# Token mixing of batches two to four by seven products of sums, with the sums of the weights made in the first batch

## The chip, the cores and the metric

The kernel runs on one core of a Trainium2 chip. The metric is the time of one execution on the device in microseconds (us). Five engines work side by side, each with a queue of its own that it takes in order: TensorE (PE in the profile; PEld are its weight loads), VectorE (DVE), ScalarE (ACT), GpSimd (POOL) and SyncE (SP), which here issues all transfers between DRAM and the on-chip memory SBUF. Matrix products are summed up in the eight banks of PSUM.

## The reference

Clustered attention for 4 batches, 8 heads, 768 tokens and 64 values a head gives `x` (4 x 768 x 512). The change concerns what follows:

```python
theta = x @ w_theta                       # 512 x 512
zr, zi = x * np.cos(theta), x * np.sin(theta)
yr = np.einsum('ts,bsd->btd', w_tok_r, zr)   # w_tok_r, w_tok_i: 768 x 768
yi = np.einsum('ts,bsd->btd', w_tok_i, zi)
u = x + yr + yi
return u + np.maximum(u @ w_ch, 0.0)      # w_ch: 512 x 512
```

## The kernel before

The first part, 447 us long, is attention: 16 pairs of heads in an order written out by hand (`todo`, `in_order`). It also turns the 64-bit weights into 32 bits (`early_weights`). The second part, the one changed, goes through the batches. It is recorded in program order, and a scheduler then sets the order on each engine.

All products are made in fp32r from a rounded part and its residue: ScalarE casts to the high part, GpSimd (or VectorE) subtracts it for the low part, and TensorE sums three products, high by high, high by low, low by high.

- `theta(b, t)`: for 128 tokens (tile t of 6), 12 products of 512 columns into bank `tp` (L659), then on VectorE `kk`, `r` (L665 to L667), a turned copy `xn` of x (L652), ScalarE's absolute value and sines (L670, L924), VectorE's products with x (L926), the casts (L929) and GpSimd's subtractions (L931). Result: zr, zi with high and low parts, 128 tokens x 512.
- `mix(b, t)` (L980): for each of four blocks of 128 channels and for r and i, three products with the high or low part of the weight tile's 768 columns, cut in two at the bank's edge, 48 products in all. y (512 channels x 768 tokens) fills six banks over the six tiles. In the last batch the columns go in parts of 256 (72 products a tile), and the last two tiles are done part by part, so that its channel stage starts early.
- `add_y` (L991 to L994): x + y on VectorE, cast and residue for u. `channel` (L1003, L1008): 8 blocks of 12 products of 384 columns, ReLU and sum on VectorE, the result to DRAM.

Theta runs two tiles ahead of mix. During the first batch also `late()` works: it brings back the weight tiles 3 to 5 (`kept`, residues L893) and turns `w_ch` into 32 bits in four pieces `wtmp` (L142 to L153, casts L165, residues L166).

Of the kernel before, what the change touches and what calls it, by code (L numbers as in the profile page):

```python
# [22 lines left out]
PW = 256  # L23
TAIL = 2
# [19 lines left out]
def kernel(  # L44
# [112 lines left out]
    def split_w(hi, lo, src, cols, new, eng, most, kept=None):  # L157

        def chunk(sl):
            w = yield from to_f32(src[:, sl], sl.stop - sl.start, new)  # L160
            yield
            if kept is not None:
                nc.sync.dma_start(out=kept[:, sl], in_=w)
                return
# [17 lines left out]
    w_d = {(t, x): dram.tile([P, S], F32, name=f"wd{t}{x}") for t in range(EARLY, NT) for x in "ri"}  # L182
# [80 lines left out]
    def f(ap):  # L263
        return ap.bitcast(F32)
# [336 lines left out]
    def first_rotation():  # L601

        xs = ma[0].tile([P, NCT, P], F32, tag="ab", name="xs")
# [3 lines left out]
        xh, xl, xn, kk, r = rotation_tiles(0, "0_0")  # L607
# [12 lines left out]
    def rotation_tiles(n, name):  # L620
        pool = ma[n % 2]
        xh = pool.tile([P, NCT, P], F32R, tag="xh", name=f"xh{name}")
# [3 lines left out]
        return xh, xl, xn, kk, pool.tile([P, DM], F32, tag="r", name=f"r{name}")  # L626
# [35 lines left out]
    def rotation_reduce(n, name, tp, kk, r):  # L662
# [3 lines left out]
        nc.vector.scalar_tensor_tensor(out=r, in0=kk, scalar=-C1, in1=tp, op0=ALU.mult, op1=ALU.add)  # L666
        nc.vector.scalar_tensor_tensor(out=r, in0=kk, scalar=-C2, in1=r, op0=ALU.mult, op1=ALU.add)  # L667
# [177 lines left out]
    pm = mctx.enter_context(tc.tile_pool(name="pm", bufs=2, space=PSUM))  # L845
    py = mctx.enter_context(tc.tile_pool(name="py", bufs=1, space=PSUM))
    mx = mctx.enter_context(tc.tile_pool(name="mx", bufs=2))
    ma.append(mctx.enter_context(tc.tile_pool(name="ma1", bufs=1)))
    mz = mctx.enter_context(tc.tile_pool(name="mz", bufs=3))
    m2 = mctx.enter_context(tc.tile_pool(name="m2", bufs=2))  # L850
    m1 = mctx.enter_context(tc.tile_pool(name="m1", bufs=1))
    m0 = mctx.enter_context(tc.tile_pool(name="m0", bufs=1))

    def mbank(name):
        return pm.tile([P, 512], F32, tag="bank", name=name)
# [10 lines left out]
    def load_x(b):  # L866
        xT = mx.tile([P, NP, S], F32, tag="xT", name=f"xT{b}")
# [4 lines left out]
        else:  # L872
            with tc.issue_after(last_load[0].ins):
# [238 lines left out]
```

## Time and profile before

| | us |
|---|---|
| median of 3 runs (780.78 to 781.37) | 780.91 |
| the profiled execution | 783.62 |
| its span in the profile | 781.8 |
| TensorE busy in it | 772.4 |
| VectorE busy | 553.1 |
| GpSimd busy | 493.3 |
| ScalarE busy | 389.2 |
| attention ends, first mix begins, near | 449.5 |
| channel stage of the first batch ends | 531.4 |

The profile shows one execution. Rows of a timeline or of the chain of waits begin with start and duration in us; a group of instructions has line, engine, operation, result and sources, count, busy time in us and the mean in ns. Busy matmuls overlap in the records, so TensorE's pace is read from the chain, where the pieces follow each other without overlap. The chain is the work that ended last, followed back.

### The profile page before, as it was taken

Reading aid. Unit: us, or ns where it says so; the run is one execution under the profiler, and the core shown is the slowest. Engines: PE = TensorE matmul, PEld = TensorE weight load, DVE = VectorE, ACT = ScalarE, POOL = GpSimd, SP = SyncE. Lnnn points to the kernel's source line nnn. Section 1 sums busy time; section 2 is a strip of 40 time slices with the busy share of each in tenths; the row PEclk is TensorE's granted clock in tenths of the full one; section 3 lists DMA queues with packets and bytes.
Section 4 is the critical chain, followed back from the end, with each engine's and each line's share of the span. In section 5 each row is a group of like instructions: output and inputs, shape, how many; then the busy total and the mean of one; then the engine's idle time right before and its main releaser. Section 6 shows DMA issues by size and latency. Waiting matters only on the chain.

```text
span 781.8 us, 14392 instructions
## 1 busy us (share of the span) xinstructions
PE 772.4 (99%) x5580; PEld 571.6 (73%) x5580; DVE 553.1 (71%) x689; ACT 389.2 (50%) x781; POOL 493.3 (63%) x289
## 2 busy tenths in 40 slices
PE   8999999999999999999998999999999999999998
PEld 6666566656666665666664588898889988899998
DVE  7788999999899989999899577854344444533322
ACT  3566766676767666666655555432333132503310
POOL 4568888989999999988986575461225112422231
PEclk9999999999999999999999999999999999999999
DMA  4123323433343334333453476124101411120001
GB/s 143 42 60 100 113 77 113 137 109 97 120 140 107 102 115 144 124 108 129 131 201 115 104 198 193 28 56 147 27 14 28 162 28 28 17 92 15 1 21 62
DMA packets 82592, 73.23 MB, mean 94 GB/s; under 512 B 59538, under 2 KB 66844, under 8 KB 82140
## 3 DMA queue, kind: packets, MB, share of 16 engines
q1 hardware_dynamic: 82524, 72.32, 31.2%
q8 instruction: 44, 0.72, 0.4%
q14 instruction: 24, 0.20, 0.1%
HBM read 56.89 MB, written 15.31 MB: 92 GB/s over the span
## 4 chain that ended last, share of the span: by engine, by line
PE 87%; DVE 6%; DMA 3%; ACT 2%; issue 1%; SPq 1%; POOL 0%; DVEq 0%; ACTq 0%
PE sc L411 26%; PE y L980 20%; PE av L559 17%; PE tp L659 6%; PE cy L1003 5%; PE m L411 4%; PE cp L1003 3%; PE sm L526 2%; PE lg L287 2%; DMA wtmp<-in_w_ch_dram 1%; PE y L1003 1%; PE lt L300 1%; DVE nm L433 1%; PE mt L441 1%; PE idle L228 1%
## 5 line engine op out<-in xcount | busy, mean ns | idle before, releaser
L487 ACT ACTIVATE at<-sc 128x384 f32<-128x384 f32 x384 | 174.0, 493 | 96.3 <-PE sc L411 52.4
L433 DVE TENSOR_REDUCE nm<-m 128x1 f32<-128x768 f32 x192 | 180.2, 947 | 26.0 <-PE m L411 24.5
L498 POOL TENSOR_TENSOR acc<-at,at 128x768 f32<-128x768 f32 x64 | 126.0, 1969 | 37.5 <-ACT at L487 37.5
L411 PE MATMUL m<-hk,hq 64*128 64x384 f32 x384 | 147.4, 384 | 0.2 <-DVE nm L433 0.2
L559 PE MATMUL av<-at,vt 128*64 128x384 f32 x768 | 146.4, 502 | 0.2 <-ACT xt L574 0.2
L498 POOL TENSOR_TENSOR acc<-acc,at 128x768 f32<-128x768 f32 x64 | 132.5, 2070 | 10.0 <-ACT at L487 8.0
L931 POOL TENSOR_TENSOR zlc<-ab,zhc 128x512 fp32r<-128x512 f32 x24 | 32.4, 1351 | 158.5 <-ACT zhc L929 157.0
L411 PE MATMUL m<-mk,mq 64*128 64x384 f32 x384 | 128.2, 334 | 0.1
L411 PE MATMUL sc<-hq,hk 64*128 64x384 f32 x384 | 116.7, 390 | 1.1 <-ACT at L487 1.1
L411 PEld LDWEIGHTS sc<-hq,hk 64*128 64x128 f32 x384 | 55.1, 183 | 63.5 <-issue 25.3
L411 PE MATMUL sc<-hq,lk 64*128 64x384 f32 x384 | 97.1, 335 | 0.0
L411 PE MATMUL sc<-mq,mk 64*128 64x384 f32 x384 | 97.0, 335 | 0.0
L411 PE MATMUL sc<-lq,hk 64*128 64x384 f32 x384 | 96.7, 335 | 0.0
L559 PEld LDWEIGHTS av<-at,vt 128*64 128x64 f32 x768 | 46.8, 137 | 59.4 <-issue 54.1
L411 PEld LDWEIGHTS m<-hk,hq 64*128 64x128 f32 x384 | 70.4, 183 | 2.0 <-DVE nm L433 1.4
L411 PEld LDWEIGHTS m<-mk,mq 64*128 64x128 f32 x384 | 71.1, 185 | 0.8 <-DVE mk L376 0.4
L665 DVE TENSOR_SCALAR kk<-tp 128x512 int32<-128x512 f32 x24 | 16.4, 685 | 76.5 <-PE tp L659 76.5
L502 DVE TENSOR_TENSOR acc<-acc,acc 128x768 f32<-128x768 f32 x30 | 63.9, 2130 | 0.0
L632 ACT CAST xh<-xT 128x512 fp32r<-128x512 f32 x23 | 14.2, 619 | 95.8 <-PE tp L659 91.6
L994 POOL TENSOR_TENSOR ul<-xT,uh 128x384 fp32r<-128x384 f32 (+1 forms) x36 | 33.5, 959 | 35.5 <-ACT uh L993 33.8
L411 PEld LDWEIGHTS sc<-mq,mk 64*128 64x128 f32 x384 | 54.3, 185 | 0.0
L411 PEld LDWEIGHTS sc<-hq,lk 64*128 64x128 f32 x384 | 54.1, 185 | 0.0
(177 smaller groups left out, 1699.3 us busy)
## 6 DMA issues: line engine op xcount, KB each, us to landing
vt<-in_v_dram SPq DMA_DIRECT2D x16, 384.0 KB
rb<-sd SPq DMA_DIRECT2D x32, 192.0 KB
xT_d<-xt SPq DMA_DIRECT2D x16, 384.0 KB
xb<-xT_d SPq DMA_DIRECT2D x96, 64.0 KB
rawq<-in_qT_dram SPq DMA_DIRECT2D x15, 384.0 KB
rawk<-in_kT_dram SPq DMA_DIRECT2D x15, 384.0 KB
w<-in_wrT_dram SPq DMA_DIRECT2D x6, 768.0 KB
xT<-xT_d SPq DMA_DIRECT2D x3, 1536.0 KB
```

The source lines that it names most:

```text
L411: nc.tensor.matmul(out, lhsT=stat[r, cols], rhs=mov[r, over], start=start, stop=stop)
L433: nc.vector.tensor_reduce(out=s["nm", a][:, j, i // 2:i // 2 + 1], in_=s["m", j][:, :, 0:HS], op=ALU.max, axis=AX.XY, negate=True)
L487: last_exp[0] = nc.scalar.activation(out=s["at", a, i][:, j], in_=s["sc", j], func=AF.Exp, scale=SCALE)
L498: last_acc[0] = nc.gpsimd.tensor_tensor(out=s["acc", a, x], in0=prev, in1=at, op=ALU.add)
L502: nc.vector.tensor_tensor(out=s["acc", a, 0], in0=s["acc", a, 0], in1=s["acc", a, 1], op=ALU.add)
L559: nc.tensor.matmul(s["av"][64 * j:64 * j + 64], lhsT=s["vt"][:, i, j, :], rhs=s["at", a, i][:, j], start=(i == 0), stop=(i == NT - 1))
L659: nc.tensor.matmul(tp, lhsT=xx[:, c, :], rhs=w_th[c][k], start=(n == 0), stop=(n == 3 * NCT - 1))
L665: nc.vector.tensor_scalar_mul(kk, tp, INV_2PI)
L931: nc.gpsimd.tensor_tensor(out=zl, in0=tr, in1=zh.bitcast(F32), op=ALU.subtract)
L980: last_mix[0] = nc.tensor.matmul(y_at(b, d, c0, c1), lhsT=zz[:, d * P:(d + 1) * P], rhs=ww[:, c0:c1], start=first and lead, stop=last, ski ...
L994: nc.gpsimd.tensor_tensor(out=ul[:, d, :], in0=x, in1=uh[:, d, :].bitcast(F32), op=ALU.subtract)
L1003: nc.tensor.matmul(cp, lhsT=w_c[d][k][:, e * P:(e + 1) * P], rhs=uu[:, d, :], start=(n == 0), stop=(n == 3 * NCT - 1), skip_group_check=True)
```

## The change

Per tile and batch the mixing is y = Wr zr + Wi zi. With channels and token columns each cut in two, it is a product of two by two blocks, and from the second batch on it is made by Strassen's seven products in place of eight. The first batch stays as it was.

- *Sums of weights.* For every weight tile, `make_forms(t)` loads the 32-bit weights from DRAM (`w_d`, now stored for all six tiles in attention), makes five sums on VectorE, seven casts on ScalarE and seven residues (five on GpSimd, two on VectorE). The seven forms (128 x 768: high and low halves of 384 columns) go where parts of the weights used up by the first batch stood. It is called for tile 4 behind the first batch's mix of tile 0, for 5 and 0 behind tile 2, for 1 and 2 behind tiles 3 and 4, for tile 3 behind the channel stage. The forms of tiles 4, 5 and 0 are also stored in DRAM and loaded in each batch (`load_forms`), tile 4 into the buffers of u, tile 5 into the place of tile 0.
- *Sums of z.* `split_z(b, t, h)` for each half h of the channels (256): three sums on VectorE, two casts, two residues on GpSimd. The second half waits in DRAM (`z_d`) until the first half's mix is done.
- *Products.* `mix_forms`: 7 forms x 3 products of 384 columns for a tile and half. Product four goes to a bank of its own, the six others to the banks of y. `add_products`: seven instructions on VectorE add them to x, once per half.
- *Channel stage.* `split_u_part` makes u's first half on GpSimd during the second half's mix, the second half behind `add_products` on VectorE; the products are taken in two steps, for the two halves. The last batch's parts of 256 columns (`PW`, `TAIL`) go.
- *Loads and buffers.* One buffer for x in place of two; theta's columns (`load_columns`) come by loads of their own; two z buffers in place of three; x of the next batch is loaded behind the channel stage.

The diff, cut to its core:

```diff
-            for w, src in ((w_r, wrT), (w_i, wiT)):
-                yield from split_w(*w[t], src[t * P:(t + 1) * P], S, raw_pair, nc.gpsimd, CKE)
+            for w, src, x in ((w_r, wrT, "r"), (w_i, wiT, "i")):
+                yield from split_w(
+                    *w[t], src[t * P:(t + 1) * P], S, raw_pair, nc.gpsimd, CKE, kept=w_d[t, x])
...
+    ORDER = (4, 3, 1, 5, 2, 6, 7)
...
+    KEPT = (4, 5, 0)
...
+    def make_forms(t):
+        raw = u_tile(f"raw{t}").rearrange("p c s -> p (c s)").bitcast(F32)
+        for x, k in enumerate("ri"):
+            nc.sync.dma_start(out=raw[:, x * S:(x + 1) * S], in_=w_d[t, k])
...
+        for x, m in enumerate(ORDER):
+            to = subs[PLACE[t][x]]
+            hi, lo = to[:, 0:HS], to[:, HS:S]
+            p, op, q = W_SUM[m]
+            src = part[:, p]
+            if op is not None:
+                src = part[:, 1] if m == 6 else sums[:, {4: 0, 3: 1, 1: 2, 7: 3}[m]]
+                nc.vector.tensor_tensor(out=src, in0=part[:, p], in1=part[:, q], op=op)
+            nc.scalar.copy(out=hi, in_=src)
+            (nc.vector if x in (1, 4) else nc.gpsimd).tensor_tensor(out=lo, in0=src, in1=f(hi), op=ALU.subtract)
+            if t in KEPT:
+                nc.sync.dma_start(out=w_f[t][:, m - 1], in_=f(to))
+
+    def load_forms(t):
+        for m in ORDER:
+            nc.sync.dma_start(out=f(forms[t][m]), in_=w_f[t][:, m - 1])
+
+    def split_z(b, t, h):
...
+            src = mzb.tile([P, 2, HD], F32, tag="zb", name=f"zb{b}_{t}")
+            nc.sync.dma_start(out=src, in_=z_d.pop((b, t)))
...
+        nc.vector.tensor_tensor(out=sums[:, 0:HD], in0=c[:, 0:HD], in1=s[:, 0:HD], op=ALU.add)
+        nc.vector.tensor_tensor(out=sums[:, HD:3 * P], in0=c[:, 0:P], in1=s[:, P:HD], op=ALU.add)
...
+        nc.vector.tensor_tensor(
+            out=parts[:, 1:n + 1:n - 1], in0=src[:, :, P:HD], in1=src[:, :, 0:P], op=ALU.subtract)
+        for cols, of in ((slice(0, 3 * P), sums), (slice(3 * P, 7 * P), src[:, :, 0:HD])):
...
+            nc.scalar.copy(out=h_, in_=of)
+            nc.gpsimd.tensor_tensor(out=l_, in0=of, in1=f(h_), op=ALU.subtract)
...
+    def mix_forms(tiles, first, last):
+        for m in ORDER:
+            cols = slice(Z_AT[m] * P, (Z_AT[m] + 1) * P)
+            for x, (t, (zh, zl)) in enumerate(tiles):
+                hi, lo = forms[t][m][:, 0:HS], forms[t][m][:, HS:S]
+                for k, (zz, ww) in enumerate(((zh, hi), (zh, lo), (zl, hi))):
+                    nc.tensor.matmul(
+                        product(m), lhsT=zz[:, cols], rhs=ww, start=first and x == k == 0,
+                        stop=last and x == len(tiles) - 1 and k == 2, skip_group_check=True)
+
+    def add_products(b, h):
...
+        add(x[:, 0:3:2], twice(4), ALU.add)
+        add(x[:, 1:4:2], twice(3), ALU.subtract)
+        add(x[:, 0:4:3], twice(1), ALU.add)
+        add(x[:, 0:4:3], y[:, 2:4, 0:HS], ALU.subtract)
+        add(x[:, 1:3], y[:, 2:4, 0:HS], ALU.add)
...
+    made = {0: (4,), 2: (5, 0), 3: (1,), 4: (2,)}
+    for t in range(NT):
+        theta(*divmod(t + AHEAD, NT))
...
+        mix(t)
+        for x in made.get(t, ()):
+            make_forms(x)
+    channel_first()
+    load_x(1)
+    make_forms(3)
...
+    for b in range(1, B):
+        load_forms(4)
+        z = split_z(b, 0, 0)
+        for t in range(NT):
+            if t + AHEAD < NT:
+                theta(b, t + AHEAD)
+            now, z = z, split_z(b, t + 1, 0) if t + 1 < NT else None
+            mix_forms([(t, now)], t == 0, t == NT - 1)
+            if t == 0:
+                load_forms(5)
+        if b + 1 < B:
+            theta(b + 1, 0)
+        z = split_z(b, 5, 1)
+        add_products(b, 0)
+        for t in (5, 4, 3, 2):
+            now, z = z, split_z(b, t - 1, 1)
+            mix_forms([(t, now)], t == 5, False)
+            if t == 5:
+                load_forms(0)
+            if t == 4:
+                split_u_part(b, 0, us, nc.gpsimd)
+            if t == 3 and b + 1 < B:
+                theta(b + 1, 1)
+        mix_forms([(1, z), (0, split_z(b, 0, 1))], False, True)
+        add_products(b, 1)
+        split_u_part(b, 1, us, nc.vector)
+        channel(b, us)
+        if b + 1 < B:
+            load_x(b + 1)
```

What the scheduler makes of it is seen in the order of the instructions. First GpSimd in the first batch, from the residues of tile 3 or 4 to those of tile 5, before (`zlc`, `zls` are the low parts of z):

```order
L931 TENSOR_TENSOR zls_3_6297<-r_3_6261,zhs_3_6296 128x512
L166 TENSOR_TENSOR wch_lo<-wtmp,wch_hi 128x512 x2
L931 TENSOR_TENSOR zlc_4_6399<-ab_4_6388,zhc_4_6398 128x512
L931 TENSOR_TENSOR zls_4_6405<-r_4_6369,zhs_4_6404 128x512
L166 TENSOR_TENSOR wch_lo<-wtmp,wch_hi 128x512
L931 TENSOR_TENSOR zlc_5_6499<-ab_5_6488,zhc_5_6498 128x512
L931 TENSOR_TENSOR zls_5_6505<-r_5_6469,zhs_5_6504 128x512
```

The same place in the changed kernel (L957 are the residues of z, L164 those of the channel weights, L1034 the forms' residues, `raw` and `sums` the weights and their sums; the results stand in the old weights' places and so bear their names):

```order
L957 TENSOR_TENSOR z_4_6437<-rab_4_6407,z_4_6437 128x512 x2
L164 TENSOR_TENSOR wch_lo<-wtmp,wch_hi 128x512
L1034 TENSOR_TENSOR wi_hi<-raw_6503,wi_hi 128x384
L1034 TENSOR_TENSOR wi_lo<-sums_6506,wi_lo 128x384
L1034 TENSOR_TENSOR wr_lo<-sums_6506,wr_lo 128x384 x2
L1034 TENSOR_TENSOR ws_6116<-raw_6533,ws_6116 128x384
L164 TENSOR_TENSOR wch_lo<-wtmp,wch_hi 128x512
L1034 TENSOR_TENSOR wr_hi<-raw_6503,wr_hi 128x384
L1034 TENSOR_TENSOR ws_6079<-sums_6536,ws_6079 128x384
L1034 TENSOR_TENSOR ws_6081<-sums_6536,ws_6081 128x384
L1034 TENSOR_TENSOR wi_hi<-sums_6536,wi_hi 128x384
L957 TENSOR_TENSOR z_5_6595<-rab_5_6565,z_5_6595 128x512 x2
```

Nine residues of forms now stand between tile 4's and tile 5's residues of z, and five more (tile 4's forms) between those of tiles 2 and 3; the second and third pieces of the channel weights have moved among them, and the fourth to behind tile 5's.

Second, VectorE at the end of the first batch's `add_y`, before (L991 the adds, L1008 the channel stage's result):

```order
L991 TENSOR_TENSOR xT_6062<-y_0_6206,xT_6062 128x384
L991 TENSOR_TENSOR xT_6062<-y_0_6206,xT_6062 128x128
L652 STREAM_TRANSPOSE xn_3_7017<-xb_6944 128x512
L991 TENSOR_TENSOR xT_6062<-y_0_6207,xT_6062 128x256 x2
L991 TENSOR_TENSOR xT_6062<-y_0_6208,xT_6062 128x128
L991 TENSOR_TENSOR xT_6062<-y_0_6208,xT_6062 128x384
L1008 SCALAR_TENSOR_TENSOR ot_0_0_6803<-cp_0_0_6790,xT_6062 128x384
```

And now (L1117 the adds, L1057 a sum of z, L1032 and L1034 sums and residues of tile 2's forms, L142 to L151 the fourth piece of the channel weights):

```order
L1117 TENSOR_TENSOR xT_6091<-y,xT_6091 128x256
L1117 TENSOR_TENSOR xT_6091<-y,xT_6091 128x384
L1057 TENSOR_TENSOR rab_1_6804<-rab_1_6804 128x2x128
L142 TENSOR_SCALAR wtmp<-wtmp 128x512
L1034 TENSOR_TENSOR wr_hi<-raw_6779,wr_hi 128x384
L1032 TENSOR_TENSOR sums_6782<-raw_6779 128x384 x4
L652 STREAM_TRANSPOSE xn_2_7093<-xb_6829 128x512
L145 TENSOR_SCALAR wtmp<-wtmp 128x512
L1032 TENSOR_TENSOR raw_6779<-raw_6779 128x384
L1034 TENSOR_TENSOR wr_lo<-sums_6782,wr_lo 128x384
L148 SCALAR_TENSOR_TENSOR wtmp<-wtmp 128x512
L151 SCALAR_TENSOR_TENSOR wtmp<-wtmp 128x512
```

The conversion of the fourth piece, which stood ahead of the adds, now follows them, among the sums of tile 2's forms.

More of the change, by code (lines that the diff above doesn't have):

```diff
@@ L22 @@
 LEAD = 10
-PW = 256
-TAIL = 2
 NEXT = 1
@@ L161, in chunk @@
             yield
-            if kept is not None:
-                nc.sync.dma_start(out=kept[:, sl], in_=w)
+            nc.sync.dma_start(out=kept[:, sl], in_=w) if kept is not None else None
+            if hi is None:
                 return
@@ L180 @@
     w_c = {}
-    w_d = {(t, x): dram.tile([P, S], F32, name=f"wd{t}{x}") for t in range(EARLY, NT) for x in "ri"}
+    w_d = {(t, x): dram.tile([P, S], F32, name=f"wd{t}{x}") for t in range(NT) for x in "ri"}
     ma = [ctx.enter_context(tc.tile_pool(name="ma0", bufs=1))]
@@ L1033 @@
-    order = [(b, t) for b in range(B) for t in range(NT)]
-    rotate(0, 0, first["r"], first["ab"], first["xn"])
-    for n in range(1, AHEAD):
-        theta(*order[n])
-    late_weights = late()
-    for n, (b, t) in enumerate(order):
-        if n + AHEAD < len(order):
-            nb, nt = order[n + AHEAD]
-            if nt == 0:
-                load_x(nb)
-            theta(nb, nt)
-        if b == 0:
-            weights_after[0] = splits[n + 1]
-            next(late_weights, None)
-        if b < B - 1 or t < NT - TAIL:
-            mix(b, t)
-            if t == NT - 1:
-                channel(b)
@@ L1052, with channel_out @@
-    u = None
-    for part in range(S // PW):
-        for t in range(NT - TAIL, NT):
-            mix(B - 1, t, (part,))
-        if u:
-            channel_part(B - 1, part - 1, u)
-        u = add_y(B - 1, part * PW, (part + 1) * PW)
-    channel_part(B - 1, S // PW - 1, u)
+                    cp, lhsT=w_c[d][w][:, e * P:(e + 1) * P], rhs=uu[:, d, :],
+                    start=k == 0 and d == 0, stop=k == 2 and d == NCT - 1, skip_group_check=True)
+    def channel_out(b, e, ch, cp):
+        c = slice(ch * HS, (ch + 1) * HS)
+        ot = m2.tile([P, HS], F32, tag="ot", name=f"ot{b}_{ch}_{e}", bufs=2)
+        nc.vector.scalar_tensor_tensor(
+            out=ot, in0=cp, scalar=0.0, in1=xts[b][:, e, c], op0=ALU.max, op1=ALU.add)
+        nc.sync.dma_start(out=out[b, e * P:(e + 1) * P, c], in_=ot)
@@ new lines, in channel_first, with channel @@
+    def channel_first():
+        us = [add_y(0, ch * HS, (ch + 1) * HS) for ch in range(2)]
+        for x in range(2 * NCT):
+            ch, e = divmod(x, NCT)
+            cp = (mbank(f"cp0_{x}") if x < 2 else y[:, x - 2])[:, 0:HS]
+            channel_products(cp, e, us[ch], range(NCT))
+            channel_out(0, e, ch, cp)
+    def channel(b, us):
+        for x in range(2 * NCT):
+            ch, e = divmod(x, NCT)
+            cp = product(ORDER[x % 7])
+            for ds in ((0, 1), (2, 3)):
+                channel_products(cp, e, us[2 * ch:2 * ch + 2], ds)
+            channel_out(b, e, ch, cp)
@@ new lines @@
+    rotate(0, 0, first["rab"], first["xn"])
+    theta(0, 1)
+    late_weights = late()
+    made = {0: (4,), 2: (5, 0), 3: (1,), 4: (2,)}
+    for t in range(NT):
+        theta(*divmod(t + AHEAD, NT))
+        weights_after[0] = splits[min(t + 1, len(splits) - 1)]
+        next(late_weights, None)
+        mix(t)
[4 more added lines that the diff above has]
+    make_forms(3)
+    us = [u_tile(f"u{x}") for x in range(4)]
+    forms[4] = {
+        m: us[x // 2].rearrange("p c s -> p (c s)")[:, x % 2 * S:(x % 2 + 1) * S] for x, m in enumerate(ORDER)}
@@ new lines @@
+    four[0] = pm[1].tile([P, 512], F32, tag="bank", name="four")
+    for b in range(1, B):
[27 more added lines that the diff above has]
+            load_x(b + 1)
```

216 lines of the change are left out of this document (125 added, 91 removed).

## The prediction

> **What bounds the kernel now.** I read the page's first two parts, then the chain of waits from 430 us on (start, duration, what), then busy time by stretch.
>
> ```profile
> PE 772.4 (99%) x5580; PEld 571.6 (73%) x5580; DVE 553.1 (71%) x689; ACT 389.2 (50%) x781; POOL 493.3 (63%) x289
> ```
> ```profile
> 516.50 0.62 PE cp L1003 x2
> ...
> 524.94 6.41 PE cy L1003 x37
> 531.35 2.76 PE tp L659 x12
> 534.11 8.41 PE y L980 x48
> ...
> 701.31 8.63 PE y L980 x72
> ...
> 735.45 20.15 PE y L980 x168
> ...
> 761.37 5.76 PE y L980 x48
> ...
> 772.89 2.88 PE cp L1003 x24
> 775.77 2.89 PE y L1003 x24
> ```
> From 516.5 us on the chain is TensorE alone, block after block: each TensorE microsecond taken away there is a microsecond of the whole. Before that, in the first batch, the chain runs through VectorE, ScalarE and DMA. The busy table by stretch (columns: time, length, PE, PEld, DVE, ACT, POOL with counts, clock, DMA share, GB/s) says why:
>
> ```profile
> 449.50:500.40 50.90, 50.90 (x278) 43.86 (x277) 39.37 (x50) 25.96 (x42) 32.51 (x19) 1.00 0.58 158
> 454.50:476.80 22.30, 22.30 (x122) 19.20 (x121) 14.37 (x13) 11.68 (x19) 22.21 (x12) 1.00 0.78 210
> ...
> 531.40:598.30 66.90, 66.90 (x362) 57.49 (x360) 31.12 (x51) 24.33 (x41) 16.38 (x14) 1.00 0.21 50
> ```
> In a later batch (last row) VectorE and GpSimd are half empty; in the first they are not, and they hinder each other. GpSimd's and VectorE's timelines, the last column of each row being what its idle time waited for:
>
> ```profile
> 456.16 1.30 POOL L931 TENSOR_TENSOR zls<-r,zhs 128x512 fp32r<-128x512 f32 x1
> 457.41 1.87 POOL L893 TENSOR_TENSOR wr_lo<-kept,wr_hi 128x768 fp32r<-128x768 f32 x1
> 459.23 2.30 POOL L893 TENSOR_TENSOR wi_lo<-kept,wi_hi 128x768 fp32r<-128x768 f32 x1
> 466.28 1.76 POOL L931 TENSOR_TENSOR zlc<-ab,zhc 128x512 fp32r<-128x512 f32 x1
> 498.93 1.47 POOL L931 TENSOR_TENSOR zls<-r,zhs 128x512 fp32r<-128x512 f32 x1
> 601.65 3.94 POOL L994 TENSOR_TENSOR ul<-xT,uh 128x384 fp32r<-128x384 f32 x4
> ```
> ```profile
> 458.03 1.80 DVE L926 TENSOR_TENSOR ab<-ab,xn 128x512 f32<-128x512 f32 x1
> 459.75 2.32 DVE L926 TENSOR_TENSOR r<-r,xn 128x512 f32<-128x512 f32 x1
> 466.80 0.68 DVE L666 SCALAR_TENSOR_TENSOR r<-kk,tp 128x512 f32<-128x512 int32 x1
> 467.51 1.07 DVE L667 SCALAR_TENSOR_TENSOR r<-kk,r 128x512 f32<-128x512 int32 x1
> 477.75 0.70 DVE L652 STREAM_TRANSPOSE xn<-xb 128x512 f32<-128x512 f32 x1
> 538.28 0.69 DVE L926 TENSOR_TENSOR ab<-ab,xn 128x512 f32<-128x512 f32 x1 [1.51 <-ACT ab L924]
> 538.89 0.69 DVE L926 TENSOR_TENSOR r<-r,xn 128x512 f32<-128x512 f32 x1
> ```
> With GpSimd idle a VectorE product takes 0.69 us, one every 0.61 (538.28, 538.89). While GpSimd runs, the same instruction takes 1.80 and 2.32 and ends 0.55 after GpSimd's own end (457.41 + 1.87 = 459.28; VectorE ends at 459.83). The next GpSimd subtraction, begun at 459.23, takes 2.30 for 1.87. So VectorE's instructions on two SBUF operands and GpSimd's subtractions exclude each other; one that reads PSUM (L666) runs through GpSimd's 466.28 piece in 0.68.
>
> The test is the stretch 454.5 to 476.8, with GpSimd busy 22.21 of 22.30. Its twelve subtractions alone would need 6 x 1.28 + 6 x 1.84 = 18.7 us (pitches from the rows above), its eight such VectorE instructions 7 x 0.60 + 0.87 = 5.1: together 23.8 against 22.3, factor 0.94. From 449.5 until tile 5's last residue (498.93 + 1.47 = 500.4) I count 27.7 + 18.5 = 46.2 against 50.9, factor 1.10. The two queues' times add up, within 0.94 to 1.10. In the Trainium skill, SBUF — State Buffer, section Who interferes with whom, the read interface is an exclusive lock between a VectorE instruction with two SBUF inputs and a GpSimd one that reads SBUF. By that rule the factor is 1, inside the two measured ones.
>
> **The change: what it takes from TensorE.** Mixing now costs 2 x 6 x 8.41 + 3 x 8.63 + 20.15 + 5.76 = 152.7 us in batches two to four. After it there are 3 batches x 12 half tiles x 21 products of 384 columns = 756. Channel products have this shape, 6.41 / 37 = 0.1732 us, so 130.9. Gain 21.8. The last batch's channel products go from six blocks of 2.88 (17.3) to 96 x 0.1732 = 16.6: gain 0.6. Sum 22.4. Thetas keep their number.
>
> **What it adds to the first batch.** Each of five `make_forms` calls ahead of the channel stage, and a sixth behind it, brings five sums and two subtractions to VectorE, five subtractions to GpSimd, seven casts to ScalarE, two loads, and, for tiles 4, 5 and 0, seven stores. ScalarE, busy 25.96 of 50.90, hides its casts.
>
> Up to tile 5's residue GpSimd then has 12 x 1.28 + 6 x 1.84 + 14 x 0.98 = 40.1 us (0.98 is 3.94 / 4), VectorE's two-operand work 24 x 0.60 + 0.87 + 19 x 0.47 + 4 x 0.34 = 25.6 (0.87, 0.47 and 0.34 are estimates by width from the 0.60). Sum 65.7: tile 5 is ready at 449.5 + 65.7 = 515.2, where now it is at 500.4 and TensorE wants it near 506. TensorE's mix of tile 5 then ends at about 524.
>
> VectorE reaches its first `add_y` only behind 12.3 us more of such work, with 4.5 more on GpSimd (two residues of tile (1, 0), a channel-weight piece, a form): 82.5 in all, 532.0; with the factors, 527.1 to 540.3. This, not TensorE, sets the channel stage.
>
> Then VectorE has the twelve adds and ten rows of the order piece above, the last two of which convert the fourth channel-weight piece. The rows for these:
>
> ```profile
> 510.41 0.74 DVE L991 TENSOR_TENSOR xT<-y,xT 128x384 f32<-128x384 f32 x2
> 511.68 1.41 DVE L991 TENSOR_TENSOR xT<-y,xT 128x256 f32<-128x256 f32 x4
> 514.48 0.75 DVE L991 TENSOR_TENSOR xT<-y,xT 128x384 f32<-128x384 f32 x2
> 515.77 1.38 DVE L991 TENSOR_TENSOR xT<-y,xT 128x256 f32<-128x256 f32 x4
> ```
> ```profile
> 482.73 0.62 ACT L165 CAST wch_hi<-wtmp 128x512 fp32r<-128x512 f32 x1
> ```
> ```profile
> 467.52 9.11 DMA wtmp<-in_w_ch_dram
> ```
> Adds 4.3, the ten rows 5.5 + 0.6 for the transpose, ScalarE's cast 0.6, and between 0 and 12 us of GpSimd's queue in between (ten forms' subtractions and tile (1, 1)'s two residues); I take half, 6.0. TensorE, in order, can do nine channel products before the tenth needs that piece: it goes on at 532.0 + 4.3 + 6.1 + 0.6 + 6.0 = 549.0 (538.1 to 563.3). Now the same point, 87 products ahead of 531.35, is at 531.35 - 87 x 0.1732 = 516.3. Lost: 32.7 us (21.8 to 47.0).
>
> SyncE's queue is in order too: the stores of forms stand ahead of this piece's load, which so goes out near 518 and, at the 9.11 us of the first such load, lands by 527: ahead of 532, hence no term. The six early stores in attention cost SyncE some microseconds among 447: nothing.
>
> **Other additions.** TensorE idles over 10 us there. In attention a short idle left this:
>
> ```profile
> 415.00:420.00 5.00, 2.60 (x21) 1.19 (x17) 4.96 (x6) 1.65 (x4) 3.40 (x2) 1.00 0.51 158
> 420.00:424.00 4.00, 4.00 (x23) 2.39 (x24) 3.93 (x4) 2.00 (x5) 3.49 (x3) 0.63 0.67 130
> 424.00:426.00 2.00, 2.00 (x18) 0.69 (x16) 2.00 (x1) 0.39 (x1) 1.40 (x1) 0.89 0.50 197
> ```
> 4 x 0.37 + 2 x 0.11 = 1.7 us of clock lost after the idle. An earlier restart, at tile 5, hides in the wait that follows; I add one, 1.7.
>
> In batches two to four the lock holds: GpSimd 12 x 2.26 + 3.7 = 30.8, VectorE some 27, of 76.7 us of TensorE a batch. `add_products` (five instructions of 0.87 and two of 0.47, 5.3 us) starts 3.1 us ahead of the half's end, product four being first; what is left hides behind a theta (2.74) and products of bank `four`, except in the last batch. 0 to 1.5 us a half; I take 2.0 in all. The last z halves are loaded behind the seven forms of tile 0 (2.75 MB), for which the rate is between
>
> ```profile
> 4.00:6.00 2.00, 1.63 (x21) 1.30 (x22) 1.34 (x7) 1.41 (x2) 0.03 (x1) 1.00 0.98 336
> 466.00:486.00 20.00, 20.00 (x109) 17.17 (x108) 14.75 (x20) 8.69 (x15) 12.26 (x8) 1.00 0.81 239
> ```
> At 336 GB/s 8.2 us, then about 2 for the half and 3 for its sums and splits, less the 10.4 us of products until it is wanted: at most 2.8 late, at least 0; I take 1.0 a batch, nearer the row of long transfers. Together 5.0 (0 to 14).
>
> Sum: +32.7 + 1.7 + 5.0 - 22.4 = +17.0. The profiled execution took 783.62 us (span 781.8), so 800.6; it lies 2.71 above the median of the runs, 780.91, and for the median I say **797.9**. Bounds: 21.8 - 22.4 = -0.6 and 47.0 + 1.7 + 14 - 22.4 = +40.3, so 780 to 821.
>
> **Rivals.** *The two queues overlap after all*, and it is faster. For it: the factor 0.94, and that the stretch has only eight VectorE instructions under the lock, where 65 come now. Against: each of the quoted collisions. VectorE alone would be at the adds in time (37.9 + 13.0 of work on 449.5: 500.4), they end at 517.2 as now, and the fourth piece comes 6.7 later, at 523.9: lost 7.6, sum 7.6 + 5.0 - 22.4 = -9.8, **771**. It decides where TensorE's tenth channel product comes ahead of 532.0 (516.3 + 22.4 - 1.7 - 5.0). Chance 0.24.
>
> *Streaming binds.* At the 239 GB/s of the second row, tile 0's forms and two z halves (3.3 MB) take 13.8 us, with 3 for the splits 6.4 beyond the 10.4: 19 us in three batches for the 3.0 above, **814**. For it: SyncE's single queue of short xb packets among the loads; against it 336. Chance 0.10.
>
> *TensorE does not get its eighth.* Every product loads its own weights:
>
> ```profile
> L1003 PEld LDWEIGHTS cy<-uh,wch_hi 128*128 128x128 f32 x72 | 12.9, 188 | 0.0
> ```
> 188 ns a load beside 173 ns a product: if loads set the pace, 756 x 0.015 = 11.3 us of the gain go, **809**. The channel blocks speak against it: same shapes, 0.1732 with a load each. The Trainium skill, TensorE: Matmul & The Clock Gate, section LDWEIGHTS, gives columns over 1.2, an estimate of 107 ns for 128; by it no load binds, by the measured 188 it nearly does. Chance 0.04.
>
> **Numbers.** Forecast 0.62, rivals 0.24, 0.10, 0.04. About 0.2% (1.6 us) is what a measurement can tell from no change. Faster: 0.24 of the first rival and 0.01 of the forecast's low end, 0.25; the same 0.03; slower 0.72. The forecast's own range is 780 to 821; the whole, 767 to 815, leaves out the first rival's lower third (under 767) and the forecast's upper end, together under 0.2.
>
> **What would show it.** Right: from 447 us to the channel stage GpSimd busy over nine tenths, VectorE's L1032 and L952 rows at 1 to 2 us, TensorE waiting ahead of tile 5's mix and longest ahead of its tenth channel product, near 549; then 21 products in 3.64 us. Wrong: that product before 532; waits of TensorE on forms or z halves in batches two to four above 14 us; products above 0.18 us.

## The result, and the profile after

The changed kernel takes 910.22 us (median of 4 runs, 907.76 to 912.74), the kernel before 780.93: ratio 1.1655, 95% interval 1.1615 to 1.1695. It is slower, as forecast, but by 129 us where 17 were forecast and 40 was the upper bound. The profiled execution took 912.74 us, span 910.9.

The page's first two parts: busy time, and the clock granted to TensorE in 40 slices of 22.8 us.

```profile
PE 802.0 (88%) x5280; PEld 591.3 (65%) x5280; DVE 681.5 (75%) x847; ACT 420.4 (46%) x843; POOL 556.2 (61%) x333
...
PEclk9999999999999999989999876799879989899889
```

TensorE has 300 instructions fewer and is busy 30 us longer, for 109 us it is not busy at all, and from 500 us on (the last 18 slices) its clock is under nine tenths in ten of them. The list of TensorE's waits from 440 us on (what waited, for what; us in total, times, longest) says where:

```profile
PE tp L659 <- DVE rab L667: 26.3, 7, 7.3
PE y L1127 <- DVE ot L1134: 18.4, 14, 7.3
PE four L1079 <- POOL zf L1064: 11.1, 14, 1.4
PE four L1079 <- ACT zf L1063: 9.3, 8, 2.5
PE cp L1127 <- ACT uh L1119: 9.0, 1, 9.0
PE cp L1127 <- ACT wch_hi L163: 8.1, 1, 8.1
PE y L1127 <- DVE xT L1088: 3.8, 1, 3.8
```

All rows of the list together are 96 us; for the kernel before they are 0.4. The two rows on `cp` are the first batch, which the prediction had; TensorE's timeline there:

```profile
545.60 1.01 PE L1127 MATMUL cp<-uh,wch_hi 128*128 128x384 f32 x2 [9.02 <-ACT uh L1119]
...
557.89 0.69 PE L1127 MATMUL cp<-uh,wch_hi 128*128 128x384 f32 x1 [8.10 <-ACT wch_hi L163]
```

The second row is the tenth channel product. It was forecast for 549.0 and comes at 557.9, inside its bounds. From there to the end of the span the forecast left 798.8 - 549.0 = 249.8 us, and the run took 353.0. So of the 112 us by which the profiled execution misses its forecast, 8.9 stand ahead of this product and 103.2 behind it, in the rest of the first channel stage and in batches two to four. There the prediction had two costs: 1.7 us for the clock after a long idle, and the 5.0 us (0 to 14) with which "Other additions" ends. Busy time in four stretches from 500 us on, the last three in that part (time, length, PE, PEld, DVE, ACT, POOL, clock, DMA share, GB/s):

```profile
500.00:550.00 50.00, 30.61 (x132) 24.72 (x130) 48.28 (x68) 23.88 (x47) 32.03 (x25) 0.81 0.65 216
550.00:600.00 50.00, 31.91 (x132) 28.42 (x133) 29.37 (x44) 13.02 (x25) 20.07 (x18) 0.75 0.49 135
...
650.00:700.00 50.00, 39.73 (x177) 35.20 (x176) 29.55 (x45) 11.63 (x20) 14.66 (x13) 0.86 0.33 90
...
800.00:850.00 50.00, 39.30 (x207) 35.34 (x205) 23.84 (x41) 10.06 (x18) 13.94 (x12) 0.98 0.58 209
```

In the first row VectorE is full, with 48 of 50 us. In the others no engine is: TensorE is busy for 32 to 40 of 50 us, VectorE for 24 to 30, the DMA engines for a third to six tenths. This is the picture of engines that wait for one another. In the channel stage of the second batch the reason can be read:

```profile
694.03 0.51 PE L1127 MATMUL y<-u,wch_hi 128*128 128x384 f32 x2
695.24 0.62 PE L1127 MATMUL y<-u,wch_hi 128*128 128x384 f32 x2 [0.70 <-DVE ot L1134]
...
697.11 0.51 PE L1127 MATMUL y<-u,wch_hi 128*128 128x384 f32 x2
698.27 0.62 PE L1127 MATMUL y<-u,wch_hi 128*128 128x384 f32 x2 [0.65 <-DVE ot L1134]
701.28 0.62 PE L1127 MATMUL y<-u,wch_hi 128*128 128x384 f32 x2 [0.65 <-DVE ot L1134]
```

A block of 12 products goes to one bank of `y`, the next block to another. Yet each block waits until VectorE has read the block before it; a block is 3.0 us where it was 2.1. The kernel before has six tiles of one bank (`tag=f"y{x}"`); the changed one allocates `y` as one tile of six banks. The full diff has that line; the prediction passed it over.

### The profile page after: what moved, and what is told of

It reads as the page before. It is cut to its first block, busy times and chain, and to the rows that moved or that the text cites. A ratio compares the mean times of both kernels' runs of the same rounds, so it can differ in the third digit from the quotient of the medians.

```text
span 910.9 us, 14439 instructions
## 1 busy us (share of the span) xinstructions
PE 802.0 (88%) x5280; PEld 591.3 (65%) x5280; DVE 681.5 (75%) x847; ACT 420.4 (46%) x843; POOL 556.2 (61%) x333
## 5 line engine op out<-in xcount | busy, mean ns | idle before, releaser
L1064 POOL TENSOR_TENSOR zf<-zt,zf 128x384 fp32r<-128x384 f32 x36 | 37.6, 1045 | 194.1 <-ACT zf L1063 194.1
L1063 ACT CAST zf<-zt 128x384 fp32r<-128x384 f32 x36 | 18.5, 514 | 149.1 <-DVE zt L1055 63.1
L659 PE MATMUL tp<-wth_hi,xh 128*128 128x512 f32 x96 | 31.9, 461 | 26.4 <-DVE rab L667 26.3
L409 PEld LDWEIGHTS sc<-lq,hk 64*128 64x128 f32 x384 | 54.7, 187 | 0.0
```

The lines of the kernel that those rows point to most:

```text
L409: nc.tensor.matmul(out, lhsT=stat[r, cols], rhs=mov[r, over], start=start, stop=stop)
L659: nc.tensor.matmul(tp, lhsT=xx[:, c, :], rhs=w_th[c][k], start=(n == 0), stop=(n == 3 * NCT - 1))
L1063: nc.scalar.copy(out=h_, in_=of)
L1064: nc.gpsimd.tensor_tensor(out=l_, in0=of, in1=f(h_), op=ALU.subtract)
```

## The experiments

Theory A: the one tile `y` makes every write wait for the last read of any bank, and each wait lowers the granted clock besides. Theory D, the prediction's: sums and residues of forms, on two engines that exclude each other, delay the first batch. Rivals: the two `ot` buffers behind SyncE's queue (B), thetas and z halves (C, F, G), an overlap of the two engines (H). Every time below is the median of 4 or 5 runs, with the ratio to the kernel before, run beside it on the same chip, and its 95% interval.

### Six tiles for y

```diff
-    y = mpool("py", space=PSUM).tile([P, 6, 512], F32, name="y")
+    py = mpool("py", space=PSUM)
+    y = [py.tile([P, 512], F32, tag=f"y{x}", name=f"y{x}") for x in range(6)]
...
-        add(x[:, 0:4:3], y[:, 2:4, 0:HS], ALU.subtract)
-        add(x[:, 1:3], y[:, 2:4, 0:HS], ALU.add)
+        add(x[:, 0], product(5), ALU.subtract)
+        add(x[:, 1], product(5), ALU.add)
+        add(x[:, 3], product(2), ALU.subtract)
+        add(x[:, 2], product(2), ALU.add)
```

> The changed kernel with the six banks of `y` as six tiles, as in the kernel before, and the two two-bank adds of `add_products` split by bank. Theory A (the one tile `y` makes TensorE wait at every channel block and every start of a half until VectorE has read the last bank, and each such wait lowers the granted clock): the 26 us of waits on `ot` and `xT` at L1127 and L1079 go, as much again of lost clock: 860 us (840 to 880), channel blocks of 12 products in under 2.3 us. Rival B (two `ot` buffers and the store behind SyncE's queue set the pace of a channel block): blocks stay near 3 us apart and the waits on `ot` stay, 900 to 912 us. Rival C (thetas and z halves bind, `y` only waits beside them): waits move to `rab` and `zf`, 895 to 910 us.

867.79 us, ratio 1.1122 (1.1061 to 1.1184): 42 us off. The last batch's channel stage on TensorE, where blocks of different banks now follow one another without a wait:

```profile
852.06 0.85 PE L1130 MATMUL y<-u,wch_hi 128*128 128x384 f32 x4
852.75 0.51 PE L1130 MATMUL y<-u,wch_lo 128*128 128x384 f32 x2
853.10 0.85 PE L1130 MATMUL y<-u,wch_hi 128*128 128x384 f32 x4
```

Four products start 0.69 us ahead of the next, 0.173 each, over the whole stage. Theory A holds, and its size too.

### The same tile in the kernel before

```diff
-        return [py.tile([P, 512], F32, tag=f"y{x}", name=f"y{x}_{b}") for x in range(NCT * S // 512)]
+        if not ys:
+            ys[-1] = py.tile([P, 6, 512], F32, tag="y", name="y")
+        return [ys[-1][:, x] for x in range(NCT * S // 512)]
...
-                    cp = py.tile([P, 512], F32, tag=f"y{x}", name=f"cy{b}_{x}")
+                    cp = ys[-1][:, x]
```

> The kernel before with its six `y` banks as one tile, nothing else. Theory A (a write to one bank of a tile waits for the read of another): in the channel stages of batches one to three and the last batch's parts each block of 12 products waits about 0.6 us for the block before, and add_y holds the first: 800 us (790 to 830). If reads and writes are held apart by bank: 781 us (779 to 783).

819.91 us, ratio 1.0471 (1.0430 to 1.0511). The allocation alone, with nothing else changed, costs 38 us, twice the 19 that were expected. TensorE's waits in the kernel before, and then with one tile:

```profile
PE cp L1003 <- ACT uh L993: 0.4, 1, 0.4
```
```profile
PE y L1005 <- DVE ot L1010: 12.5, 10, 3.5
PE cp L1005 <- ACT uh L995: 8.3, 6, 2.3
PE y L982 <- DVE ot L1010: 2.0, 3, 0.7
PE tp L659 <- DVE ot L1010: 0.9, 3, 0.3
```

The waits grow by 23.3 us and the profiled execution by 36.3 (783.62 to 819.87): a microsecond of waiting costs 1.56. The rest is slower products: the same 5580 keep TensorE busy for 785.6 us instead of 772.4, and its granted clock from 445 us on is 0.98 instead of 1.00.

### No ot buffers

```diff
-        ot = m2.tile([P, HS], F32, tag="ot", name=f"ot{b}_{ch}_{e}", bufs=2)
+        ot = xts[b][:, e, c]
```

> The changed kernel without `ot` buffers: `channel_out` writes the sum into the slice of `xT` that it has read, and the store to DRAM reads it from there. Theory A (one tile `y`): TensorE still waits about 0.6 us at each block, the time that VectorE takes with the sum; blocks come from 3.0 us apart to 2.7; 900 us (890 to 912). Rival B (the `ot` buffers bind): blocks of 2.1 us, 4 x 8 blocks x 0.9 us and some clock gained, 870 to 885 us.

908.24 us, ratio 1.1614 (1.1584 to 1.1644), the same as the changed kernel. In the last batch:

```profile
896.23 0.61 PE L1127 MATMUL y<-u,wch_hi 128*128 128x384 f32 x2 [0.65 <-DVE xT L1134]
```

The same 0.65 us, now on the write into `xT`. Rival B falls: while `y` is one tile, the buffers behind it decide nothing.

### Forms without sums and residues, alone and with six tiles

```diff
-                nc.vector.tensor_tensor(out=src, in0=part[:, p], in1=part[:, q], op=op)
+                src = part[:, p]
             nc.scalar.copy(out=hi, in_=src)
-            (nc.vector if x in (1, 4) else nc.gpsimd).tensor_tensor(out=lo, in0=src, in1=f(hi), op=ALU.subtract)
+            if PLACE[t][x] >= 24:
+                nc.scalar.copy(out=lo, in_=src)
```

> The changed kernel without VectorE's sums and without the subtractions in `make_forms`: every form's first half is ScalarE's copy of one raw quarter, its second half what the tile held (for the four spare tiles a copy); so the weights are not the sums of the reference. Theory D (the forms' two-operand work on VectorE and GpSimd, which exclude each other, delays the first batch by 33 us or more): the first `add_y` comes from 543 to 517 us or earlier, the tenth channel product from 558 to 530 or earlier, 880 us (872 to 892), batches two to four as long as in the changed kernel. Rival E (the first batch is held by the loads and stores of the forms or by ScalarE): the tenth channel product stays behind 545, over 895 us.

> Both edits at once: six tiles for `y`, and `make_forms` without sums and residues (so the weights are not the sums of the reference). If the first batch's delay and the one tile `y` are two separate losses, 867.8 - 33 = 835 us (825 to 845). If the one hid part of the other, 845 to 865; if what the first batch leaves idle makes the rest worse, under 825.

877.17 us (1.1213, 1.1159 to 1.1267) and 833.41 us (1.0688, 1.0654 to 1.0723). The first, at the first batch's channel stage:

```profile
526.68 2.29 PE L1126 MATMUL cp<-uh,wch_hi 128*128 128x384 f32 x6 [6.17 <-ACT uh L1118]
...
531.36 0.69 PE L1126 MATMUL cp<-uh,wch_hi 128*128 128x384 f32 x1 [1.43 <-ACT wch_hi L163]
```

The tenth channel product comes 26.5 us earlier, at 531.4 instead of 557.9, with the loads, stores and casts of the forms still there. So theory D holds for 26.5 us of the 41.6 that the first batch loses (516.3 to 557.9), and rival E falls as the main cause. The other 15.1 us stay without sums and residues. The kernel further below that makes no forms in its first batch (two plain batches, with six tiles) has its tenth channel product at 519.1, so all but 2.8 us go when the forms are made elsewhere and `y` has six tiles; what the casts, the loads and stores and the single tile have of the rest was not taken apart. The two losses are separate: 33.1 us of forms' work with one tile, 34.4 with six.

### Residues of forms and z halves on VectorE

In the kernel with six tiles:

```diff
-            (nc.vector if x in (1, 4) else nc.gpsimd).tensor_tensor(out=lo, in0=src, in1=f(hi), op=ALU.subtract)
+            nc.vector.tensor_tensor(out=lo, in0=src, in1=f(hi), op=ALU.subtract)
...
-            nc.gpsimd.tensor_tensor(out=l_, in0=of, in1=f(h_), op=ALU.subtract)
+            nc.vector.tensor_tensor(out=l_, in0=of, in1=f(h_), op=ALU.subtract)
```

> Six tiles for `y`, and the residues of all forms and of all z halves computed by VectorE instead of GpSimd. Theory D (VectorE's two-operand instructions and GpSimd's subtractions exclude each other, so that VectorE's 0.47 us takes the place of 0.98): the tenth channel product comes some 10 us earlier than 557, GpSimd's 36 times 2.3 us in batches two to four become 36 times 1.1: 850 us (838 to 860). Rival H (the two engines overlap and VectorE's length binds): the tenth channel product later than 560, batches two to four longer, 875 to 890.

838.71 us, ratio 1.0735 (1.0688 to 1.0783): 29 us off, by giving the fuller engine more to do. VectorE's timeline in the changed kernel, with GpSimd beside it, and then with GpSimd's part moved (four sums; a residue; two products of `rab`):

```profile
510.90 1.37 DVE L1034 TENSOR_TENSOR wr_hi<-raw,wr_hi 128x384 fp32r<-128x384 f32 x1
512.19 2.78 DVE L1032 TENSOR_TENSOR sums<-raw 128x384 f32<-128x384 f32 x4
514.90 2.90 DVE L952 TENSOR_TENSOR rab<-rab,xn 128x512 f32<-128x512 f32 x2
```
```profile
507.47 1.95 DVE L1033 TENSOR_TENSOR sums<-raw 128x384 f32<-128x384 f32 x4
509.35 0.54 DVE L1035 TENSOR_TENSOR ws<-raw,ws 128x384 fp32r<-128x384 f32 x1
510.76 1.28 DVE L953 TENSOR_TENSOR rab<-rab,xn 128x512 f32<-128x512 f32 x2
```

The same four sums take 1.95 us instead of 2.78, a residue 0.54 instead of 1.37, two products 1.28 instead of 2.90. GpSimd is busy beside the first rows from 510.5 to 517.2 us but for two gaps of 1.5 and 0.3 us; beside the second rows it is idle. TensorE's timeline there:

```profile
533.28 1.01 PE L1130 MATMUL cp<-uh,wch_hi 128*128 128x384 f32 x2 [5.38 <-ACT uh L1122]
...
545.12 4.21 PE L1130 MATMUL y<-uh,wch_hi 128*128 128x384 f32 x12 [7.63 <-ACT uh L1122]
```

The products that follow the second wait start 12 us earlier than with six tiles alone (557.1). Rival H falls: if the two queues overlapped, more work on VectorE would have come later, not earlier. By the Trainium skill, SBUF — State Buffer, section Who interferes with whom, the two engines share a port pair under an exclusive lock; these rows agree with it.

### Two zt buffers, output in place

With six tiles. `split_z` has one buffer `zt` for its sums, and there was no SBUF for a second; the output in place frees 3 KB a partition.

```diff
-    mzt = mpool("mzt")
+    mzt = mpool("mzt", 2)
...
-        ot = m2.tile([P, HS], F32, tag="ot", name=f"ot{b}_{ch}_{e}", bufs=2)
+        ot = xts[b][:, e, c]
```

> Six tiles for `y`, the output written into `xT` in place of the two `ot` buffers, and, in the room that this leaves, two buffers instead of one for the sums `zt` of a z half. Theory F (TensorE's 15 us of waits on `zf` and 7 on `ot` with six tiles come from `split_z` that runs without overlap, VectorE's sums of the next half waiting for GpSimd's residue of this one): those waits fall under 8 us, 850 us (840 to 858). Rival G (VectorE's own order, thetas and adds in front, makes z halves late): waits stay, 860 to 870.

> Six tiles for `y`, output in place, two `zt`, and all residues of forms and z halves on VectorE. If the 21 us of the second and third edit and the 29 us of the fourth are separate losses, 867.8 - 21 - 29 = 818 us (810 to 826). If both took the same waits on `zf` away, 830 to 840.

The first gives 846.57 us (1.0850, 1.0829 to 1.0871): 21 off, for two edits that no run separates. TensorE's waits fall from 69 to 57 us, those on `ot` to nothing, those on `zf` from 14.7 only to 12.0. So the gain is there, but not by the route that theory F gave it: the waits on `zf` stay over 8, as rival G said, those on `rab` fall from 18.3 to 9.7, and those on `xT` grow from 6.9 to 13.0. What one buffer costs VectorE can be seen in its groups in batches two to four of the changed kernel (busy, mean ns, then idle time and what ended it):

```profile
L1054 DVE TENSOR_TENSOR zt<-zb 128x256 f32<-128x256 f32 x18 | 16.2, 899 | 32.6 <-DMA zb<-zd 17.3 <-POOL zf L1064 15.3
...
L1054 DVE TENSOR_TENSOR zt<-rab 128x256 f32<-128x256 f32 x16 | 12.8, 799 | 20.2 <-POOL zf L1064 19.5
```

For 34.8 us VectorE stands ahead of a sum until GpSimd has read the sums of the half before, with thetas, adds and `ot` queued behind it. With two buffers this is down to 0.9 us, but ahead of the halves that come from DRAM VectorE then stands 25.5 us for their loads, where it stood 17.3. With the residues on VectorE too: 827.31 us (1.0583, 1.0562 to 1.0604), between what two separate losses (818) and one common loss (830 or more) would give. They share some 9 us.

### Forms made in a later batch

Batches up to `PLAIN` are mixed as the first; `make_forms` runs in the last of them.

```diff
-    for t in range(NT):
-        theta(*divmod(t + AHEAD, NT))
+    for n in range(PLAIN * NT):
+        b, t = divmod(n, NT)
+        theta(*divmod(n + AHEAD, NT))
...
-        mix(t)
-        for x in made.get(t, ()):
-            make_forms(x)
-    channel_first()
+        mix(b, t)
+        if b == PLAIN - 1:
+            for x in made.get(t, ()):
+                make_forms(x)
+        if t == NT - 1:
+            channel_first(b)
+            load_x(b + 1)
```

> The kernel of six tiles, output in place and two `zt`, with the second batch mixed plainly as the first, and the forms made in the second batch; only batches three and four use the seven products. The first batch then has the work that it had in the kernel before. Theory D (forms made in the first batch delay it because VectorE and GpSimd also split weights there): the first batch ends as before, tenth channel product near 516, the second has room for the forms; TensorE's gain falls from 22.4 to 15.1, and a third of what is lost in batches two to four goes: 803 us (790 to 820). Rival I (forms delay whichever batch makes them): TensorE waits 20 us or more in the second batch, over 825.

> The kernel with the second batch mixed plainly and the forms made there, with all residues of forms and z halves on VectorE. Theory D (the two engines exclude each other, and the shorter instruction wins): the 15 us of waits on `rab`, most of them behind the forms in the second batch, fall by half or more, and batches three and four lose the waits on `zf`: 796 us (785 to 804). Rival H (VectorE, in order, is now the longest engine of these batches): 808 to 822.

> As the one before, with three plain batches and the forms made in the third: only the last batch, which has four thetas instead of six, uses the seven products. Theory J (the gain is real where VectorE has few thetas: with six tiles the last batch took 69 to 71 us, in the kernel before 80.0): 781 - 10 for the last batch + 0 to 15 for the forms in the third: 778 us (770 to 787), the first version near or below the kernel before. Rival (what a batch of seven products gains is lost in any batch that makes forms): over 788.

All three have six tiles, output in place and two `zt`. Two plain batches: 815.71 us (1.0457, 1.0438 to 1.0476); with residues on VectorE 795.25 (1.0165, 1.0150 to 1.0181); three plain batches, residues on VectorE: 794.55 (1.0162, 1.0146 to 1.0178). With the residues on VectorE the forms fit under a batch that has no weights to split: TensorE waits 0.5 us in the second batch. With those on GpSimd it still waits 12.0 there, 9.6 of them at once, so something of rival I stays. And seven products for two batches are worth no more than for one. Of the second kernel, TensorE's longest waits:

```profile
PE y L1081 <- ACT zf L1065: 6.5, 4, 2.5
PE tp L659 <- DVE rab L667: 2.2, 1, 2.2
PE four L1081 <- DVE zf L1066: 2.1, 2, 1.4
```

Its two batches of seven products are longer than the two that they replace. VectorE's last sums of the second channel stage come late there, behind sums and residues of forms, so the time is counted on TensorE: from the theta behind that stage to the end of the span it is 174.2 us (620.45 to 794.6), in the kernel before 167.0 (614.79 to 781.8). Theory J, a gain of 10 us in a last batch, falls as it was put. In the second kernel the last batch takes 68.2 us from last sum to last sum, but the one before it 98.3, where the kernel before has 80.0 and 83.6. And in the third kernel, where only the last batch has seven products, it takes 88.1 us, counted on TensorE in the same way (704.03 to 792.1), in the kernel before 83.4 (698.39 to 781.8).

### Forms spread, and the cast in attention

Forms of tiles 4, 5 and 0 made in the second batch through the four spare tiles, those of 1, 2 and 3 in the third.

```diff
-            to = subs[PLACE[t][x]]
+            to = spares[x % 4] if t in KEPT else subs[PLACE[t][x]]
...
-    made = {0: (4,), 2: (5, 0), 3: (1,), 4: (2,)}
+    made = {6: 4, 8: 5, 10: 0, 14: 1, 16: 2}
```

> As the kernel with three plain batches, and the forms spread: those of tiles 4, 5 and 0, which go to DRAM anyway, are made in the second batch through the four spare tiles, only those of tiles 1, 2 and 3 in the third. Theory J (the last batch's 9.7 us of waits on `zf` and `xT` come from VectorE, which is 47 of 50 us busy with forms just before): these waits fall under 4 us, the third batch loses nothing, 784 us (777 to 790). Rival K (the waits belong to the first batch that uses the seven products, whenever the forms are made, since its z halves start behind thetas and adds on VectorE): they stay, 790 to 796.

791.62 us (1.0123, 1.0104 to 1.0143). This kernel lacks one load of tile 0's forms, so that its last batch's first half tile is multiplied with another tile's forms. Rival K is the nearer: TensorE waits 0.3 us in the third batch now, but 5.6 us of waits stay in the last.

Its timeline, like that of every variant of the changed kernel so far, also has a wait of TensorE in attention that the kernel before does not have. In the changed kernel, ScalarE's row and then TensorE's:

```profile
399.46 0.62 ACT L632 CAST xh<-xT 128x512 fp32r<-128x512 f32 x1 [7.04 <-DMA xT<-xT_d]
```
```profile
400.52 0.82 PE L409 MATMUL sc<-hq,hk 64*128 64x384 f32 x2 [5.70 <-ACT at L485]
```

A cast for theta (0, 1), which stood at 411.8 in the kernel before, now stands ahead of exponentials of the attention and waits for a load. Attention's last products (`sm`) begin at 449.2 instead of 445.2. The cast put later:

```diff
-        nc.scalar.copy(out=xh, in_=xs)
+        with behind(cast_after):
+            nc.scalar.copy(out=xh, in_=xs)
...
-        rotation_parts(xs, xh, xl, last_out[0] if late else None)
+        rotation_parts(xs, xh, xl, last_out[0] if late else None, every_exp[-32] if n == 1 else None)
```

> The changed kernel with one order more: ScalarE's cast `xh` of theta (0, 1), line 632, comes at or behind the place that it had in the kernel before, 16 rows later among the exponentials of the attention. Theory L (that cast waits 7.0 us on ScalarE for the DMA of `xT` and holds the exponentials that TensorE waits for, so that the attention ends 4 us later than before): the wait of 5.7 us at 400 goes, the first mix begins near 447, 906 us (903 to 908). If the lateness of the attention's end comes from something else: 910 (908 to 913).

> The kernel of three plain batches with spread forms, with tile 0's forms loaded ahead of the last batch (in the kernel with spread forms that load was missing, so that its first half tile read another tile's forms) and the cast of theta (0, 1) later as in the run above. Theory L takes 4 us off 791.6: 788 us (784 to 791). Theory K (the waits in the first batch of seven products stay whatever is made ahead of it) keeps it above the kernel before; under 782 would show it wrong.

> The kernel of two plain batches with residues on VectorE, and the cast of theta (0, 1) later: 4 us off 795.25, 791 us (787 to 794); if the later start was hidden by waits in the second and third batch, 794 to 796.

907.24 us in the changed kernel (1.1629, 1.1611 to 1.1647), 789.25 in the one with spread forms (1.0112, 1.0098 to 1.0126), which also has its missing load again, 792.58 with two plain batches (1.0155, 1.0132 to 1.0178): 3, 2 and 3 us. Each interval overlaps that of the kernel without this edit, so the times alone do not show the gain; the traces do. ScalarE's row in the first of them has no wait:

```profile
404.64 0.61 ACT L635 CAST xh<-xT 128x512 fp32r<-128x512 f32 x1
```

`sm` begins at 446.5, so 2.7 of the 4.0 us come from this cast. The kernel at 789.25 is the fastest that was found, and it is slower than the one before, by 1.1%. Its waits on TensorE from 447 us on:

```profile
PE y L1084 <- ACT zf L1068: 2.6, 2, 2.2
PE four L1084 <- DVE xT L1093: 2.1, 1, 2.1
PE four L1084 <- DVE zf L1069: 0.8, 1, 0.8
```

They stand in the last batch, whose saving on TensorE is 8.8 us: 51.8 of mixing (152.7 less 12 x 8.41) against 252 products in 43.6, and 0.6 in the channel stage. With the granted clock, 0.89 from 720 to 750 us, they use up more than that. The theta behind the third channel stage, in the kernel before and then in this one:

```profile
698.39 1.09 PE L659 MATMUL tp<-wth_hi,xh 128*128 128x512 f32 x4
```
```profile
699.67 1.08 PE L662 MATMUL tp<-wth_hi,xh 128*128 128x512 f32 x4
```

From there to the end of the span it is 83.4 us before and 86.3 now. Of the 4.2 us between the two spans (781.8 and 786.0) 1.3 stand ahead of the last batch and 2.9 in it.

## Why the prediction was wrong

*The first batch: the kind of loss was right, its time in part by luck.* It was forecast to lose 32.7 us (21.8 to 47.0) because VectorE's and GpSimd's two-operand work adds up. It lost 557.9 - 516.3 = 41.6, and 26.5 of them go with that work; the run with the residues moved to VectorE decides against the first rival, an overlap. But the step in the middle missed its range: VectorE's first add was forecast for 532.0 (527.1 to 540.3), and it came 11 us later.

```profile
543.07 4.05 DVE L1117 TENSOR_TENSOR xT<-y,xT 128x384 f32<-128x384 f32 x12
```

Of these 11 us 2.7 to 4.0 are the attention's late end. The rest was not taken apart; VectorE was full, with 48.3 of 50 us from 500 on, and its other instructions, which the sum left out (`kk`, `xn`, the first steps of the channel weights), stand in the same queue. From the first add to the tenth product it then took 14.8 us where 17.0 were forecast, and so the product came back inside its bounds. GpSimd was not busy for nine tenths, as the prediction wanted to see, but for 65.7 of the 98.6 us from 447 to the channel stage. In the rows above L1032 took 0.7 us each, less than the 1 to 2 named, L952 1.45.

*TensorE's gain: the pace was right, the saving did not come out.* Where the granted clock is full, products follow at 0.173 us, also in the rows of the experiments, so weight loads set no pace (that rival falls). Products above 0.18, a sign of being wrong, came in the rows of the last section, with a granted clock of 0.50. But the saving of some 7 us a batch is less than the waits and the clock that come with it: even in the best version a batch of seven products takes 2.9 us more than one of eight.

*"Other additions", 5.0 (0 to 14): the step that failed.* It had `add_products` at 2.0 and late z halves at 3.0; behind the tenth product the run took 103 us more than the forecast. Three parts are shown, and they were found by runs, not by the prediction:

- One tile `y`, 42 us. The prediction let what is left of `add_products` hide "behind a theta (2.74) and products of bank `four`", and let channel blocks follow one another as before. That needs each bank to be free when its own reader is done; with one tile none is until the last is.
- `split_z` in series and the residues on GpSimd, 40 us on top of six tiles (867.79 to 827.31), of which some 11 lie in the first batch. The prediction compared sums of busy time, 30.8 and 27 against 76.7 us a batch, and found room. But a half tile is needed every 3.64 us of products, through sum, cast and residue on three engines with one buffer: it is the chain that is too long, not any engine that is full. The runs do not divide the 40 us among the chain's links; the load of a z half from DRAM is one of them (below).
- The granted clock. The prediction had 1.7 us for one restart. In the profiled execution the waits are 96 us, and besides TensorE is busy for 802.0 us where 772.4 - 22.4 = 750.0 would do: 52 us more for the products, at a granted clock of 0.87 from 500 us on. With 4.0 in attention these are the overrun of 151.5 against 783.6 - 22.4 = 761.2. In the kernel before with one tile the same relation stands alone: 36.3 for 23.3 of waits.

These parts do not lead back to the forecast: 827.31 is still 29 us above 797.9, and what came off after that came for the most part by making the forms in a later batch.

*The rival that streaming binds: not the main cause, but not wrong.* No wait of TensorE on forms is in the list, and with the same loads the kernel came down to 827.31. But the point named to tell it, over 14 us of waits on forms or z halves in batches two to four, was met (20.4 us on `zf` alone), in part by its own cause. In each of these batches the last two z halves were loaded behind the forms of tile 0, and VectorE stood 4.2, 2.6 and 1.9 us for one of them; in the second batch:

```profile
657.76 0.43 DVE L1054 TENSOR_TENSOR zt<-zb 128x256 f32<-128x256 f32 x1 [4.17 <-DMA zb<-zd]
```

The prediction took 1.0 us a batch for it. No run changed the loads, so their share stays open.

*"Nothing" for the early stores* may be right, but the attention still changed: one cast was moved ahead of exponentials by the scheduler, 2.7 us. The order of ScalarE's instructions shows that move (row 533 instead of 557); it was not looked at there.

## What to carry to other kernels

When a change re-allocates buffers, read what each tile holds as closely as what is computed: a tile of six banks is one thing to wait for, and banks that are meant to overlap must be tiles of their own. When a stage becomes shorter for the bounding engine, compare the chain that feeds one piece of it with the new length of that piece, not the sums of busy time with the whole. And price a wait of TensorE at about one and a half times its length, since the products beside it were slower too in both kernels: 36.3 us for 23.3 of waits, and 148 for 96.

## What the runs showed of the hardware

Half pace without a long wait. In the changed kernel TensorE has only waits of about a microsecond here, and then its products follow at 0.96 / 3 = 0.32 us instead of 0.173, with a granted clock of 0.50 from 665 to 670 us:

```profile
661.37 0.44 PE L1079 MATMUL four<-wi_hi,zf 128*128 128x384 f32 x1 [0.81 <-POOL zf L1064]
663.00 0.61 PE L1079 MATMUL four<-ws,zf 128*128 128x384 f32 x2 [1.01 <-ACT zf L1063]
664.78 0.69 PE L1079 MATMUL four<-ws,zf 128*128 128x384 f32 x1 [0.82 <-POOL zf L1064]
...
665.59 1.16 PE L1079 MATMUL y<-wr_hi,zf 128*128 128x384 f32 x3
666.55 1.16 PE L1079 MATMUL y<-ws,zf 128*128 128x384 f32 x3
```

The Trainium skill, TensorE: Matmul & The Clock Gate, section What's actually happening, has the clock halved after an idle window of about 3.4 us. The half pace agrees with these rows; the length does not, if the window is taken as one unbroken wait: the longest wait in the 14 us ahead is 1.1 us, and the last four, of 0.6 to 1.0 us within 6 us, leave TensorE busy for 2.35 of the 5 us from 660 on.

The Trainium skill, Perfetto Trace Analysis, section Matmuls, advises to rotate independent groups of products through different PSUM banks, so that reading one overlaps the next. The changed kernel does rotate, and did not overlap: TensorE waited 0.65 us at each block. The overlap came only with a tile for each bank.
